# Attention and a token/channel mixer on one core: q and k loaded with 18 tokens per partition, one transfer per four heads

## The chip, the cores and the metric

The kernel runs on one core of one Trainium2 chip. The metric is the device time of one execution in microseconds, given as the median of the runs of a kernel. The profile records one more execution; its span, from the first to the last instruction, is a little shorter than its device time.

## The reference

```python
# B = 8, H = 8, S = 576, D = 64; d_tok = 256, d_ch = 1536; all inputs and the output are float32
scores = 1/sqrt(D) * q @ k.T                       # per batch and head
bias   = -(cum[i] - cum[j]),  cum = cumsum(max(s, 0))
scores = where(j > i, -1e9, scores + min(bias, 0))
attn   = softmax(scores);  x = attn @ v            # x: (8, 576, 512) once the heads are side by side
h = relu(x^T @ w_tok1) @ w_tok2;   u = x + h^T     # mixes tokens
out = u + relu(u @ w_ch1) @ w_ch2                  # mixes channels
```

## The kernel before

**Tiling.** The batches are done one after the other. In a batch the eight heads are taken as two groups of four ("quads", qd = 0, 1). Four heads with 32 rows each fill the 128 partitions: a head's 64 columns are cast to bf16, two neighbouring columns are read as one fp32 word, and VectorE's 32x32 block transpose of these words (line 617) puts 32 words on 32 partitions, with the tokens along the free axis. TensorE then forms the scores with matmuls on 32 rows, two for each head and block (line 638, the two halves of each word). ScalarE takes the exponential (657), VectorE masks the diagonal blocks (662, 670), TensorE multiplies with v (692), VectorE normalises (699, 704). The bias enters as exp(cum), multiplied into v (line 553, on GpSimd from batch 1 on). Only neighbouring blocks of 128 tokens are multiplied; a check at the end selects a general path if the data don't allow that, and for it ScalarE squares and sums all of q and k (line 579, tile `junk`). For batches 0 and 1 that check loads q and k a second time (`stage_sq`), so there are 40 quad loads in all.

After the attention of a batch come the token mixer (`tok`: lines 759, 780, and the transposes of u: on TensorE at 805 with copies at 813 and 815 for batches 0 and 1, as DMA transposes at 796 from batch 2 on) and the channel mixer (`chan`: 833, its eviction with ReLU on ScalarE at 840 or VectorE at 842, then 851, the sum at 862, the store at 867 and 870).

**The loads.** `load_quad` (line 568) brings q or k of four heads in fp32 into one of four `qkf` buffers. With R = 2 a partition gets two neighbouring tokens (512 bytes) at a time, nine times, so each head is one DMA over 32 partitions with 288 runs of 512 bytes. Heads 0 and 1 are issued on SP (`load_op`, chained in order), heads 2 and 3 on ScalarE's queue (`load_op2`, chained likewise). A load waits for its `qkf` buffer, that is for the cast (591, 593 or 595, into one of four `qkn` buffers) of the load four before it; a cast in turn waits for its `qkn` buffer, which the transpose and, from batch 2 on, the square have to leave. v comes on SP, five DMAs a batch, in runs of 256 bytes (line 544), into two `vf` buffers. The weights come through GpSimd's queue, with a cast in flight (716). SP also carries the stores and the DMA transposes.

**What sets the order.** `Plan` takes all operations with assumed costs, simulates them on the engines with one number for the DMA time of a load, and emits each engine's instructions in the order of the planned starts. Each engine, and each issuing queue, then runs its own list strictly in order. An instruction that waits holds up everything behind it on that engine. Where the plan sees TensorE idle in its first 95 us, `fills` puts in matmuls on zeros (line 937), to keep TensorE's clock up.

Of the kernel before, what the change touches and what calls it, by code (L numbers as in the profile page):

```python
# [213 lines left out]
def c_act(n, bias=False):  # L214
    occ = 0.07 + n * 0.000833 + (0.093 if bias else 0.0)
    return occ, occ + 0.22
# [7 lines left out]
def c_pool(n, per=0.0022):  # L224
    occ = 0.10 + n * per
    return occ, occ + 0.25
# [111 lines left out]
def kernel(  # L338
# [12 lines left out]
    nc = tc.nc  # L351

    B, H, S, D = q.shape
# [8 lines left out]
    LAG = 2.0  # L362
    WARM = 95.0
    TOK = 2.0
    R = 2

    const = ctx.enter_context(tc.tile_pool(name="const", bufs=1))
    fast_ctx = ExitStack()
# [50 lines left out]
    P = Plan()  # L419
    last = [None]  # L420

    def load_op(fn, key, us):

        last[0] = P.op({"SP": (0.42, 0, fn)}, writes=key, prio=1, dma=us, after=last[0])

    last2 = [None]

    def load_op2(fn, key, us):

        last2[0] = P.op({"ACT": (0.42, 0, fn)}, writes=key, prio=0, dma=us, after=last2[0])  # L430


    nc.vector.memset(zero[:, :], 0.0)  # L433
# [20 lines left out]
    for i in range(1, 3):  # L454
        P.op({"DVE": (1.0, 1.2, lambda i=i: pads(nc.vector, i)), "POOL": (1.6, 1.8, lambda i=i: pads(nc.gpsimd, i))},
             writes=[("pad", i)], prio=40)
    P.op({"DVE": (0.6, 0.8, lambda: pads2(nc.vector)), "POOL": (1.0, 1.2, lambda: pads2(nc.gpsimd))},
         writes=["padw"], prio=41)
    P.op({"DVE": (0.3, 0.5, lambda: pads3(nc.vector, 1)), "POOL": (0.5, 0.7, lambda: pads3(nc.gpsimd, 1))},
         writes=["padv"], prio=42)  # L460
# [15 lines left out]
    def act(n, fn, bias=False):  # L476
# [4 lines left out]
         reads=["s"], writes=["sr"], prio=-1)  # L481
    P.op({"DVE": (1.3, 1.6, lambda: nc.vector.tensor_tensor_scan(
        out=cum[:, :], data0=one_sb[:, :], data1=s_sb[:, :], initial=0.0, op0=ALU.mult, op1=ALU.add))},
        reads=["sr"], writes=["cum"], prio=-1)
    P.op(dve(1, lambda: nc.vector.tensor_scalar(
        out=half[:, :], in0=cum[:, S - 1 : S], scalar1=-0.5, scalar2=None, op0=ALU.mult)),
        reads=["cum"], writes=["half"], prio=-1)
    P.op(act(576, lambda: nc.scalar.activation(
        out=wn[:, 0:S], in_=cum[:, :], func=AF.Exp, bias=half[:, 0:1], scale=1.0), True),
        reads=["half", "cum"], writes=["wn"], prio=-1)  # L490
    bw = Buf(r_mx, False)

    def w_tr():
# [6 lines left out]
        out=wT[:, :, :].rearrange("p c e -> p (c e)"), in_=bw.t[:, 0:384])),  # L500
        reads=[(bw, 0)], writes=["wT"], prio=-1)
# [18 lines left out]
        out=pre[:, :], data0=one_sb[:, :], data1=wn[:, 0:S], initial=0.0, op0=ALU.mult, op1=ALU.add))},  # L520
        reads=["wn"], writes=["pre"], prio=50)
# [44 lines left out]
    qkn, castop = {}, {}  # L566

    def load_quad(src, b, qd):
        f = Buf(r_qf)
        for g in (0, 2, 1, 3):  # L570
            on, eng = (load_op, nc.sync) if g < 2 else (load_op2, nc.scalar)
            on(lambda g=g, eng=eng: eng.dma_start(  # L572
                out=f.t[32 * g : 32 * g + 32, :].rearrange("p (k n) -> p k n", n=R * D),
                in_=src[b, 4 * qd + g, :, :].rearrange("(k p r) d -> p k (r d)", p=32, r=R)),
                [(f, g)], S / R * 0.027 / 16)
        return f

    def square(src, reads, col):
        P.op({"ACT": (1.2, 1.6, lambda: nc.scalar.activation(  # L579
            out=junk[:, :], in_=src.t[:, :], func=AF.Square, accum_out=sq[:, col : col + 1]))},  # L580
            reads=reads, writes=[("sq", col)], prio=60)

    def stage_qk(b, qd):
        for i, src in enumerate((k, q)):
            n = Buf(r_qn)
            qkn[(b, qd, i)] = n
            f = load_quad(src, b, qd)

            def cast(e, f=f, n=n):
                if e == 0:  # L590
                    nc.gpsimd.tensor_copy(out=n.t[:, :], in_=f.t[:, :])  # L591
                elif e == 1:
                    nc.vector.tensor_copy(out=n.t[:, :], in_=f.t[:, :])
                else:
                    nc.scalar.copy(out=n.t[:, :], in_=f.t[:, :])
            alts = {"POOL": (*c_pool(1152, 0.0010), lambda cast=cast: cast(0))}
            if b == 0 and (qd, i) != (1, 0):
                alts["DVE"] = (0.82, 1.04, lambda cast=cast: cast(1))
                alts["ACT"] = (*c_act(1152), lambda cast=cast: cast(2))
            castop[(b, qd, i)] = P.op(alts, reads=[(f, g) for g in range(4)], writes=[(n, 0)],  # L600
                                      prio=b * 10 + 4 * qd if b else 0)
            if b >= 2:
                square(n, [(n, 0)], (b * 2 + qd) * 2 + i)

    def stage_sq(b, qd):
        for i, src in enumerate((k, q)):
            f = load_quad(src, b, qd)
            square(f, [(f, g) for g in range(4)], (b * 2 + qd) * 2 + i)

    xbuf = {}  # L610

    def quad(b, qd):
        pads = [("pad", 1)] if b == 0 and qd == 1 else []
        qT, kT = Buf(r_qT), Buf(r_kT)
        for i, dst in ((0, kT), (1, qT)):
            n = qkn[(b, qd, i)]
            P.op(dve(576, lambda n=n, dst=dst: nc.vector.transpose(  # L617
                out=dst.t[:, 0:S, :].rearrange("d t e -> d (t e)").bitcast(FP32).rearrange(
                    "d (k p r) -> d k r p", p=32, r=R),
                in_=n.t[:, :].bitcast(FP32))), reads=[(n, 0)] + (pads if i == 0 else []), writes=[(dst, 0)], prio=1)  # L620
# [198 lines left out]
    def chan(b, u, us, uT):  # L819
# [26 lines left out]
        for ci, c in enumerate((4, 0, 1, 2, 3) if odd else (0, 1, 2, 3)):  # L846
# [24 lines left out]
            P.op({"SP": (0.45 if c < NJ - 1 else 0.9, 0, st)}, reads=[(o, 0)], prio=0, dma=128 * 0.088 / 16)  # L871

    stage_qk(0, 0)
    stage_v(0)
    stage_qk(0, 1)
    load_tok()
    stage_qk(1, 0)
    for i in range(4):
        load_ch1(i)
# [9 lines left out]
    for b in range(2):  # L889
        for qd in range(2):  # L890
            stage_sq(b, qd)
    for b in range(B):
        for qd in range(2):
# [5 lines left out]
        out=bad[:, 4:], in0=sq[:, :], scalar1=21.0, scalar2=None, op0=ALU.is_gt)),  # L899
        reads=[("sq", i) for i in range(NSQ)] + ["bad0"], writes=["bad"], prio=50)  # L900
# [3 lines left out]
         reads=["bad"], writes=[(bf, 0)], prio=(100, 0))  # L904
# [17 lines left out]
    for o in [o for o in order if o.eng == "PE"]:  # L922
# [3 lines left out]
        while t1 - t0 > 0.06:  # L926
            n = min(512, max(128, int((t1 - t0) * 2400)))
# [5 lines left out]
            if not slots:  # L933
                break
            f = Op()
            f.start, f.idx = t0, 0
            f.fn = lambda t=r.tiles[slots[0]], n=n: nc.tensor.matmul(  # L937
                out=t[:, 0:n], lhsT=zero[:, 0:128], rhs=zero[:, 0:n], start=True, stop=True)
# [47 lines left out]
```

## Time and profile before

| | us |
|---|---|
| median of 3 runs | 357.3 (356.89 to 360.31) |
| the profiled execution: its time | 357.3 |
| its span | 355.4, mean granted TensorE clock 0.945 |
| TensorE busy | 311.4, of it 35.6 in fills (line 937) in the windows of 20 us |
| VectorE / ScalarE / GpSimd busy | 196.1 / 159.8 / 86.9 |
| cast on GpSimd, L591, x29 | 34.8, 1220 ns each |
| block transposes, L617, x32 | 24.4, 771 ns (kT) and 756 ns (qT) each |
| q and k loads: DMAs | 160 of 144 KB, median 4.5 to 5.0 us from issue to landing |
| v loads | 32 of 256 KB and 8 of 128 KB, 6.9 and 6.4 us |

The profiled execution's time and the median of the runs agree. Busy times are of work alone: an engine that waits, or whose queue holds a DMA issue that waits, is counted as idle. "ACTq" and "SPq" in an answer are the issuing queues of ScalarE and SP; an issue that stands there is an instruction in that engine's list.

### The profile page before, as it was taken

The page shows a single profiled execution, that of the slowest core. Times are in us where ns is not written, and L with a number is a line of the kernel's source. Part 1 is how long each engine was busy: PE and PEld are TensorE (multiplying, and loading weights), DVE is VectorE, ACT ScalarE, POOL GpSimd, SP SyncE. Part 2 cuts the span into 40 slices and gives each one's busy share as a digit, 9 for nine tenths or more (in the row PEclk, how much of TensorE's full clock was granted, in tenths as well). Part 3 has the DMA queues.
Part 4 walks back from the last instruction along what each step waited for, and adds up shares of the span by engine and source line. Part 5 has one row for each costly group of instructions (what it writes and reads, how often), then busy time and mean ns, then how long its engine had stood idle before and what let it go on. Part 6 is the DMA issues. An engine that isn't in the chain of part 4 may idle for free.

```text
span 355.4 us, 6731 instructions
## 1 busy us (share of the span) xinstructions
PE 311.4 (88%) x2611; PEld 169.8 (48%) x2611; DVE 196.1 (55%) x422; ACT 159.8 (45%) x251; POOL 86.9 (24%) x110
## 2 busy tenths in 40 slices
PE   5896815999998499795999999999999999999992
PEld 1354414845555264342445754444467454546640
DVE  5576321738799288381196739587954454441021
ACT  0254104825562571633444745479467316414700
POOL 3167046603362092020620262025000000000000
PEclk9699686999999699898999999999999999999999
DMA  9999999379989969999059926986420231033021
GB/s 193 212 195 215 206 215 210 64 161 228 202 142 224 165 136 185 190 188 234 9 88 209 228 70 130 260 228 156 90 76 0 47 103 62 3 88 104 3 89 66
DMA packets 109640, 50.45 MB, mean 142 GB/s; under 512 B 55904, under 2 KB 104416, under 8 KB 109600
## 3 DMA queue, kind: packets, MB, share of 16 engines
q1 hardware_dynamic: 81872, 34.37, 47.1%
q10 hardware_dynamic: 24320, 11.80, 17.4%
q0 software_dynamic: 3408, 3.77, 6.3%
q8 instruction: 22, 0.36, 0.5%
q14 instruction: 18, 0.15, 0.2%
HBM read 40.71 MB, written 9.44 MB: 141 GB/s over the span
## 4 chain that ended last, share of the span: by engine, by line
PE 53%; DMA 13%; DVE 5%; SPq 4%; ACT 2%; issue 2%; POOL 1%; ACTq 0%; DVEq 0%; POOLq 0%
PE pmx L851 21%; PE pmx L833 21%; DMA vf<-in_v_dram 10%; DMA qkf<-in_k_dram 3%; PE pmx L759 3%; PE pav L692 3%; SPq L544 3%; PE psc L638 3%; PE pmx L780 2%; ACT junk L579 1%; DVE E L662 1%; DVE E L670 1%; SPq L572 1%; ACT E L657 1%; DVE kT L617 1%
## 5 line engine op out<-in xcount | busy, mean ns | idle before, releaser
L657 ACT ACTIVATE E<-psc 128x1024 bf16<-128x1024 f32 x64 | 62.0, 1021 | 46.0 <-PE psc L638 37.4
L833 PEld LDWEIGHTS <-wc 128*128 128x128 bf16 x624 | 59.8, 100 | 45.5 <-issue 16.2
L833 PE MATMUL pmx<-uTb,wc 128*128 128x320 bf16 x384 | 58.4, 305 | 6.9 <-ACT gb L840 6.3
L591 POOL CAST qkn<-qkf 128x1152 bf16<-128x1152 f32 x29 | 34.8, 1220 | 91.2 <-ACT E L657 36.1
L851 PE MATMUL pmx<-wc,gb 128*128 128x512 bf16 x240 | 56.8, 388 | 0.0
L833 PE MATMUL pmx<-uTa,wc 128*128 128x512 bf16 (+1 forms) x240 | 47.5, 348 | 4.4 <-ACT ga L840 3.8
L553 POOL TENSOR_TENSOR vp<-vf,wT 128x512 bf16<-128x512 f32 (+1 forms) x35 | 37.1, 1081 | 53.4 <-PE pav L692 22.0
L851 PE MATMUL pmx<-wc,ga 128*128 128x512 bf16 x192 | 45.2, 379 | 0.1
L662 DVE TENSOR_TENSOR E<-E,keep 128x512 bf16<-128x512 bf16 x64 | 37.2, 584 | 14.2 <-ACT E L657 13.8
L579 ACT ACTIVATE junk<-qkn 128x1152 bf16<-128x1152 bf16 x24 | 27.9, 1163 | 35.7 <-DMA vf<-in_v_dram 13.5
L840 ACT ACTIVATE gb<-pmx 128x320 bf16<-128x320 f32 x64 | 27.7, 437 | 29.8 <-PE pmx L833 22.0
L692 PEld LDWEIGHTS <-E 128*128 128x128 bf16 x576 | 26.2, 98 | 20.8 <-issue 5.1
L851 PEld LDWEIGHTS <-gb 128*128 128x128 bf16 x240 | 22.9, 99 | 26.5 <-issue 2.3
L692 PE MATMUL pav<-vp,E 128*128 128x65 bf16 x540 | 27.8, 195 | 7.9 <-DVE E L662 3.1
L937 PE MATMUL pmx<-zero 128*128 128x512 bf16 (+5 forms) x114 | 32.2, 427 | 1.2 <-DVE zero L433 1.2
L704 DVE TENSOR_TENSOR x<-pav,rc 128x320 bf16<-128x320 f32 x60 | 29.5, 491 | 1.9
L840 ACT ACTIVATE ga<-pmx 128x512 bf16<-128x512 f32 (+1 forms) x39 | 19.4, 504 | 20.3 <-PE pmx L833 19.7
L851 PEld LDWEIGHTS <-ga 128*128 128x128 bf16 x192 | 17.7, 98 | 19.8 <-issue 0.9
L699 DVE RECIPROCAL rc<-pav 128x5 f32<-128x5 f32 x60 | 11.2, 187 | 24.6 <-PE pav L692 24.3
L638 PE MATMUL psc<-qT,kT 32*128 32x256 bf16 (+2 forms) x640 | 23.1, 253 | 0.1
L862 DVE TENSOR_TENSOR of<-pmx,ua 128x512 f32<-128x512 f32 x16 | 11.0, 690 | 21.7 <-PE pmx L851 14.8
L842 DVE TENSOR_SCALAR ga<-pmx 128x512 bf16<-128x512 f32 (+1 forms) x21 | 12.3, 595 | 18.7 <-PE pmx L833 18.7
(82 smaller groups left out, 255.6 us busy)
## 6 DMA issues: line engine op xcount, KB each, us to landing
vf<-in_v_dram SPq DMA_DIRECT2D x32, 256.0 KB, 6.9
out_dram<-of SPq DMA_DIRECT2D x32, 256.0 KB, 2.4
qkf<-in_k_dram ACTq DMA_DIRECT2D x40, 144.0 KB, 5.0
qkf<-in_k_dram SPq DMA_DIRECT2D x40, 144.0 KB, 4.7
qkf<-in_q_dram ACTq DMA_DIRECT2D x40, 144.0 KB, 4.5
qkf<-in_q_dram SPq DMA_DIRECT2D x40, 144.0 KB, 4.7
wc<-in_moe_w_ch_dram POOLq DMA_DIRECT2D x8, 384.0 KB, 11.7
vf<-in_v_dram SPq DMA_DIRECT2D x8, 128.0 KB, 6.4
```

The costliest lines, as they stand in the source:

```text
L553: eng.tensor_tensor(out=vp.t[p0 : p0 + n, c, :, 0:D], in0=vf.t[p0 : p0 + n, c, :, :], in1=wT[p0 : p0 + n, cw, b * H : b * H + H].unsqueeze ...
L579: P.op({"ACT": (1.2, 1.6, lambda: nc.scalar.activation(out=junk[:, :], in_=src.t[:, :], func=AF.Square, accum_out=sq[:, col : col + 1]))}, ...
L591: nc.gpsimd.tensor_copy(out=n.t[:, :], in_=f.t[:, :])
L638: nc.tensor.matmul(out=pss[g // 2].t[:, g % 2, c0 : c0 + z - a], lhsT=kT.t[rows, j0 : j0 + 128, e], rhs=qT.t[rows, a:z, e], start=(e == 0) ...
L657: nc.scalar.activation(out=E.t[:, :, gi * 512 : gi * 512 + 512], in_=ps.t[:, :, :], func=AF.Exp, scale=0.125)
L662: nc.vector.tensor_tensor(out=o, in0=o, in1=keep[:, :].unsqueeze(1).unsqueeze(1).to_broadcast([128, 2, 2, 128]), op=ALU.mult)
L692: nc.tensor.matmul(out=o[:, ic, 0 : D + 1], lhsT=E.t[:, hh, d0 : d0 + 128], rhs=vp.t[:, jc, h + hh, 0 : D + 1], start=(jc == j_lo), stop=( ...
L704: nc.vector.tensor_tensor(out=x.t[:, :, (h + hh) * D : (h + hh + 1) * D], in0=o[:, :, 0:D], in1=rc.t[:, :].unsqueeze(2).to_broadcast([128, ...
L833: nc.tensor.matmul(out=pm.t[:, 0 : e - a], lhsT=wc1[:, m, cc * 128 : cc * 128 + 128], rhs=uT.t[:, m, a:e], start=(m == 0), stop=(m == NMC ...
L840: lambda cc=cc, pm=pm, a=a, e=e: nc.scalar.activation(out=g.t[:, cc, a:e], in_=pm.t[:, 0 : e - a], func=AF.Relu),
L851: nc.tensor.matmul(out=pm.t[:, :], lhsT=g.t[:, cc, c * 128 : c * 128 + 128], rhs=wc2[:, cc, :], start=(cc == 0), stop=(cc == NCC - 1))
L937: f.fn = lambda t=r.tiles[slots[0]], n=n: nc.tensor.matmul(out=t[:, 0:n], lhsT=zero[:, 0:128], rhs=zero[:, 0:n], start=True, stop=True)
```

## The change

R becomes 18: a partition gets 18 neighbouring tokens of one head, 4608 bytes in one run, and 32 partitions hold a head. The four heads of a quad are then 128 partitions of one contiguous piece of DRAM, and the load is one DMA, on SP. The issues on ScalarE's queue and `load_op2` go. The transpose's output pattern, which is written in terms of R, follows: within a block of 32 tokens it wrote every second word (8 bytes apart), and it now writes every 18th (72 bytes apart). What lies in `kT` and `qT` afterwards is the same as before. The planner is told 1.52 us of DMA time for a quad (128 x 0.19 / 16) where four times 0.486 us stood, and ScalarE's list has no issues.

```diff
-    R = 2
+    R = 18
...
-    last2 = [None]
-
-    def load_op2(fn, key, us):
-
-        last2[0] = P.op({"ACT": (0.42, 0, fn)}, writes=key, prio=0, dma=us, after=last2[0])
-
...
     def load_quad(src, b, qd):
         f = Buf(r_qf)
-        for g in (0, 2, 1, 3):
-            on, eng = (load_op, nc.sync) if g < 2 else (load_op2, nc.scalar)
-            on(lambda g=g, eng=eng: eng.dma_start(
-                out=f.t[32 * g : 32 * g + 32, :].rearrange("p (k n) -> p k n", n=R * D),
-                in_=src[b, 4 * qd + g, :, :].rearrange("(k p r) d -> p k (r d)", p=32, r=R)),
-                [(f, g)], S / R * 0.027 / 16)
+        load_op(lambda: nc.sync.dma_start(
+            out=f.t[:, :], in_=src[b, 4 * qd : 4 * qd + 4, :, :].rearrange("g (p r) d -> (g p) (r d)", r=R)),
+            [(f, 0)], 128 * 0.19 / 16)
         return f
...
-            castop[(b, qd, i)] = P.op(alts, reads=[(f, g) for g in range(4)], writes=[(n, 0)],
+            castop[(b, qd, i)] = P.op(alts, reads=[(f, 0)], writes=[(n, 0)],
...
-            square(f, [(f, g) for g in range(4)], (b * 2 + qd) * 2 + i)
+            square(f, [(f, 0)], (b * 2 + qd) * 2 + i)
```

The planner orders anew with these numbers. On each engine the instruction counts of the main path change as follows: the fills on TensorE go from 125 to 93; ScalarE loses its 80 issues, and takes 9 evictions of L842's kind and 3 of L770's kind from VectorE; VectorE's one cast goes to GpSimd; SP has 40 issues for q and k in place of 80. The order on TensorE changes in places, its other work does not.

## The prediction

> **What bounds the kernel now.** I read the page first, then TensorE's waits from 40 to 180 us, then ScalarE's timeline at the places where these waits point.
>
> The page's slices: TensorE, its granted clock, and the DMA engines, 8.9 us to a digit.
>
> ```profile
> PE   5896815999998499795999999999999999999992
> ...
> PEclk9699686999999699898999999999999999999999
> DMA  9999999379989969999059926986420231033021
> ```
>
> From slice 20 (178 us) on TensorE is busy at full clock until the end; nothing there can be won by feeding it better. The loss lies before: digits of 1, 4 and 5 with a clock of 6 to 8 beside them. The DMA engines are busy for most of the first 165 us, but the next view says that a transfer is not what TensorE itself waits for.
>
> TensorE's waits from 40 to 180 us (total us, times, longest):
>
> ```profile
> PE pmx L805 <- ACT uTa L813: 10.9, 1, 10.9
> PE pmx L833 <- ACT gb L840: 6.3, 2, 5.2
> PE pmx L833 <- ACT ga L840: 3.8, 1, 3.8
> PE pav L692 <- DVE x L704: 3.0, 3, 2.7
> ```
>
> Nearly all are waits for a copy on ScalarE that empties PSUM. ScalarE is only 45% busy, so why are the copies late? Its timeline (start, length, idle time ahead in brackets; ACTq is an issue on ScalarE's own queue):
>
> ```profile
> 39.88 13.17 ACTq L572 DMA_DIRECT2D qkf<-in_k_dram  x2
> 54.38 1.95 ACTq L572 DMA_DIRECT2D qkf<-in_q_dram  x2
> 56.43 2.05 ACT L813 COPY uTa<-pmx 128x512 bf16<-128x512 bf16 x4 [16.03 <-DMA qkf<-in_k_dram]
> ...
> 119.33 0.32 ACTq L572 DMA_DIRECT2D qkf<-in_k_dram  x1
> 119.69 1.16 ACT L579 ACTIVATE junk<-qkn 128x1152 bf16<-128x1152 bf16 x1 [5.69 <-DMA vf<-in_v_dram]
> ...
> 163.39 0.83 ACTq L572 DMA_DIRECT2D qkf<-in_q_dram  x2
> 164.26 1.16 ACT L579 ACTIVATE junk<-qkn 128x1152 bf16<-128x1152 bf16 x1 [6.19 <-DMA out_dram<-of]
> 165.42 1.55 ACT L840 ACTIVATE ga<-pmx 128x512 bf16<-128x512 f32 x3
> ```
>
> The four copies of uTa stand in ScalarE's list behind four issues of q and k loads. These take or wait from 39.88 to 56.33 us, and the copies start at 56.43, though TensorE had written the data at about 46. At 113 to 121 and at 162 to 166 the same happens: an issue that waits for its buffer stands in front of the gb and ga evictions. At 145 to 148 the issue at 145.72 stands in front of the exponential at 146.08, from which the x of the fourth row follows. So what bounds the first half is loads that wait inside an engine whose next work TensorE needs.
>
> **The change part by part.** All sums are made against the span of 355.4 us; the execution's time is 357.3, 1.9 more, and equals the median of the runs.
>
> *ScalarE's issues go.* The gaps behind them are 10.9, 6.3, 2.7 (the long one of the fourth row) and 3.8 us, 23.7 in all. The copies themselves remain: in each of the five places about 0.5 us (0.44 for gb, 0.60 for ga and uTa) passes before TensorE can go on, so 23.7 - 2.7 = 21. What is late next? At 46 us the matmuls L833 need wc1; the gate issue on SP, which waits for the first part of wc2, ran at 41.2 and wc1 was issued ahead of wc2, so the weights are there. The v of batch 1 was multiplied by 54.9 us for a product that TensorE reached at 78, and the casts of batch 2's first quad were done by 62.6 for scores at 91: 11 us less leaves both early. At 116 the v of the next product was ready at 104 for 134. So I find nothing late within the gain.
>
> *The clock.* After these gaps TensorE ran at a granted 0.67 (57 to 62 us), 0.61 (122 to 126), 0.66 (148 to 153) and 0.72 (166 to 172). The loss is 5 x 0.33 + 4 x 0.39 + 5 x 0.34 + 6 x 0.28 = 6.6 us. I count 5 as won, since some gaps will stay.
>
> *Fills.* 32 fewer. Ten of them are before the first scores, where 23 took 7.36 us (0.32 each), 22 mostly between 84 and 98 us, where 9 took 1.94 (0.216 each): 3.2 + 4.8 = 8 us. A fill costs nothing where the work behind it isn't ready, so the bounds are 0 and 8; TensorE hardly waited right behind the fills there (0.23 us), which speaks for the upper end. I take 6.
>
> *SP.* It issued 80 loads for 311 to 1562 ns each and now issues 40. The waits that ScalarE's queue carried stand on SP already, for the same buffers (heads 0 and 1 wait with heads 2 and 3), so SP gets no new one; behind a waiting load stand, as before, v, the stores and the DMA transposes of u. But the mutual order changes (a store of batch 0 now stands between the k and the q load of a quad), and a load on a single queue passes behind v's packets with all four heads. I charge 2 us, bounds 0 and 13 (half of the waits removed come back here).
>
> *Packets.* The rows that price them (packets, MB, share of 16 engines): the page's ScalarE queue, only q and k; and SP's queue from 322 to 355 us, stores of 2 KB with small packets.
>
> ```profile
> q10 hardware_dynamic: 24320, 11.80, 17.4%
> ...
> q1 hardware_dynamic: 1578, 1.97, 18.2%
> ```
>
> 0.174 x 16 x 355.4 / 24320 = 41 ns for one of 512 bytes, so a quad costs 1152 x 41 / 16 = 2.9 us of all engines. In the second row 0.182 x 16 x 33 = 96 us went to 896 packets of 2 KB (and 682 small ones), 107 ns at most; by bytes a packet of 4608 is 241 ns, a quad 128 x 241 / 16 = 1.9 us. Between 1.9 (near rows of large packets, taken) and 2.9 (no better by bytes) the 40 quads save 40 to 0 us of DMA time. None of it is on TensorE's path as shown above, so it enters at 0. Its cover is the lead of the loads over their use; if that is gone, it is worth up to 1 us a quad.
>
> *VectorE's transposes.* Same instruction, same elements, but writes 72 bytes apart in place of 8. No VectorE row has such a stride. The rows that bound it:
>
> ```profile
> L617 DVE STREAM_TRANSPOSE kT<-qkn x16: 737/772/781, 8.4 to 264.7; 128x576 f32<-128x576 f32 x16
> ...
> L561 POOL CAST vp<-wT 128x32 bf16<-128x32 f32 x8 | 2.5, 325 | 15.4 <-DVE wT L499 8.1 <-PE pav L692 6.2 <-PE pmx L692 1.0
> L563 POOL CAST vp<-wT 64x8 bf16<-64x8 f32 x8 | 2.0, 244 | 0.3
> ```
>
> From below, 0.77 us as now; a faster one is excluded, since VectorE's dense fp32 row at 553 (0.69 us for 512 elements) is no quicker an element. From above, GpSimd's two small casts write 132 bytes apart: (325 - 244) / (32 - 8) = 3.4 ns an element, and 576 x 3.4 + 0.17 = 2.1 us. Another engine, but the only rows with a stride like this. I take the middle, 1.4, because one end has the right instruction and the other the right stride: 32 x 0.63 = 20 us more on VectorE, which is 55% busy. The chain of waits has a kT or qT transpose at four places (183.07, 216.71, 233.41, 234.18), 4 x 0.63 = 2.5 us; with some crowding where VectorE is busy for 16 of 20 us (80 to 120), 4 us. Bounds: 0, and 32 x 1.35 = 43 if every one at 2.1 us is exposed.
>
> The Trainium skill speaks against this part: "SBUF — State Buffer", § Door 1, says that consecutive accesses within one 16-byte line go at full bandwidth, that at least two hits on a line are needed, and that an access to a new line each time pays a penalty. The old pattern has two words in a line and the new one has one. The trace shows 0.77 us for the old pattern, which agrees, and nothing for the new one. The page gives no size. Without that rule this term would be 0 and the forecast 4 us lower.
>
> The same skill speaks against a gain from the packets: "DMA: Bandwidth & Descriptors", § Specifications, has 512 bytes as the least transfer for line rate, so 4608 would save nothing of DMA time. The two rows above, 12.5 bytes a nanosecond against at least 19, differ from it. Since the term is 0 in the sum, both give the same forecast.
>
> *Sum:* 355.4 - 21 - 5 - 6 + 2 + 4 = 329.4 span, + 1.9 = **331 us**.
>
> **The rivals.**
>
> *B, the waits move.* The late thing is in truth the buffers (GpSimd's casts waited 47.7 us in all for loads and what stands before them), and with ScalarE free TensorE runs into the next wait, for a score or a v, or for a store that stands behind a load on SP. For it: the DMA engines are busy in nearly every slice up to 165 us. Against: the lead of 11 to 30 us found above. Price: half of the 26 us of gaps and clock come back, 331 + 13 = 344.
>
> *C, slower: VectorE's transposes.* At 2.1 us and with none hidden, 43 us in place of the 4: 331 - 4 + 43 = 370. It decides when (357.3 - 331 + 4) / 32 = 0.95 us more are exposed for each, that is from 1.7 us with no cover. For it: kT and qT have two buffers each, the transposes stand in one list with masks and normalisation, and TensorE's product waits on these. Against: VectorE is idle for 45% of the span and only four transposes are on the chain.
>
> *D, no change.* The planner's new order only trades one gap for another, for the same 355 to 359 us. For it: everything after 178 us is TensorE at full speed. Against: this needs 26 us of new waits in a stretch of 130 us.
>
> **How the numbers follow.** A 0.66, B 0.18, C 0.11, D 0.05. The time is A's, 331. Below, all bounds in its favour: 355.4 - 23.7 - 6.6 - 8 = 317.1 span, 319 us; I go to 317 for the startup. Above, B with a little more, 347; C and D lie outside. A and B are faster by over 1% (the three runs before spread over about 1%, so less can't be told from no change): faster 0.84, same 0.05, slower 0.11.
>
> **What would show it.** Right: no issues in ScalarE's list; TensorE's 10.9 us wait for uTa gone, the slices before 178 us without a 1; a granted clock above 0.945; L617 between 0.8 and 2.1 us; the loads of q and k landing no later after issue than 5 us. Wrong: TensorE waiting as long at the same places for scores or v (B), VectorE's kT or qT among TensorE's longest waits with L617 over 1.7 us (C), or a store or a DMA transpose on SP that waits behind a load.

## The result and the profile after

| | us |
|---|---|
| before, median | 357.1 (356.73 to 360.31) |
| after, median | 323.1 (321.15 to 323.81) |
| estimated ratio | 0.902, 95% interval 0.896 to 0.909 (the two medians alone: 0.905) |
| the profiled execution: time, span | 323.8, 322.0 |
| mean granted clock | 0.985 (0.945 before) |

34 us were gained where 26 were forecast; 323 lies inside the range. Line numbers after the edit are 6 to 9 lower: 617 is now 608, 638 is 629, 657 is 648, 813 is 804, 840 is 831, 937 is 928.

The page's slices, 8.05 us to a digit:

```profile
PE   6986989998899899997999999999999999999991
...
PEclk9799799999999999999999999999999999999998
DMA  7999988999995479402992387605101610141032
```

Up to the last slice the 1, the 4 and the 5s of TensorE are gone, and its clock falls only twice early on. TensorE's waits from 40 to 180 us (total, times, longest), the four longest:

```profile
PE pav L683 <- DVE E L661: 1.5, 2, 0.8
PE pav L683 <- DVE x L695: 1.3, 3, 0.5
PE pmx L824 <- DVE ga L833: 1.2, 2, 0.9
PE psc L629 <- DVE qT L608: 0.9, 2, 0.6
```

No wait for ScalarE is left, the longest is 0.9 us where it was 10.9, and every one of the four is for VectorE. ScalarE's timeline around the uTa copies, first the last h of before, then after, with no issue in it:

```profile
39.80 0.60 ACT L769 ACTIVATE h<-pmx 128x512 bf16<-128x512 f32 x1 [0.47 <-PE pmx L759]
```

```profile
33.56 0.60 ACT L760 ACTIVATE h<-pmx 128x512 bf16<-128x512 f32 x1 [0.47 <-PE pmx L750]
38.29 2.26 ACT L804 COPY uTa<-pmx 128x512 bf16<-128x512 bf16 x4 [4.14 <-PE pmx L796]
40.75 0.38 ACT L831 ACTIVATE ga<-pmx 128x256 bf16<-128x256 f32 x1 [0.20 <-PE pmx L824]
```

The copies start 4.7 us after the start of the last h and wait for TensorE (796); before, they started 16.6 us after it (39.80 to 56.43) and waited for a load.

The start, from which the prediction had read only the fills, gained too. The fills ahead of the first scores, and the first scores, before and after, from TensorE's timelines:

```profile
11.15 7.36 PE L937 MATMUL pmx<-zero 128*128 128x512 bf16 x23
18.44 1.09 PE L638 MATMUL psc<-qT,kT 32*128 32x256 bf16 x20
```

```profile
7.97 4.33 PE L928 MATMUL pmx<-zero 128*128 128x512 bf16 x12
12.23 1.08 PE L629 MATMUL psc<-qT,kT 32*128 32x256 bf16 x20
```

And ScalarE's first 10 us before:

```profile
0.76 0.89 ACTq L572 DMA_DIRECT2D qkf<-in_k_dram  x2
1.67 0.98 ACTq L572 DMA_DIRECT2D qkf<-in_q_dram  x2
3.91 0.97 ACTq L572 DMA_DIRECT2D qkf<-in_k_dram  x2
6.43 1.67 ACTq L572 DMA_DIRECT2D qkf<-in_q_dram  x2
8.13 1.28 ACT L488 ACT_TABLE_LOAD   x1 [8.13 <-DMA qkf<-in_k_dram]
9.43 0.78 ACT L488 ACTIVATE wn<-cum,half 64x576 f32<-64x576 f32 x1
```

Eight issues stood ahead of the table load and of the exponential of cum. It is the same stall as in the middle. It is not the whole gain: of the 6.2 us, 3.2 pass before these fills begin (11.15 against 7.97), and 3.0 are the fills themselves (23 in 7.36 us, 12 in 4.33), which the prediction had counted.

The two costs, from the tile answer for kT, the queue table and the chain of waits (before's chain is the last fence):

```profile
L608 DVE STREAM_TRANSPOSE kT<-qkn x16: 1235/1249/1260, 6.7 to 231.0; 128x576 f32<-128x576 f32 x16
```

```profile
q1 hardware_dynamic: 63312, 46.17, 51.2%
...
PE 65%; DVE 28%; issue 2%; ACT 2%; DMA 1%; SPq 0%; DVEq 0%
```

```profile
PE 53%; DMA 13%; DVE 5%; SPq 4%; ACT 2%; issue 2%; POOL 1%; ACTq 0%; DVEq 0%; POOLq 0%
```

A transpose takes 1.25 us where it took 0.77. VectorE now has 28% of the chain, where it had 5%; DMA has 1%, where it had 13%; the shares of before add up to only 80%, so they are compared roughly. One sign that the prediction had named for being right fails: the loads land 5.4 and 5.8 us after their issue, not within 5.

### The profile page after: what moved, and what is told of

Its sections match the earlier page's. It is cut to its first block, busy times and chain, and to the rows that moved or that the text cites. A ratio compares the mean times of both kernels' runs of the same rounds, so it can differ in the third digit from the quotient of the medians.

```text
span 322.0 us, 6476 instructions
## 1 busy us (share of the span) xinstructions
PE 297.7 (92%) x2579; PEld 164.3 (51%) x2579; DVE 199.4 (62%) x409; ACT 165.1 (51%) x263; POOL 88.2 (27%) x111
## 3 DMA queue, kind: packets, MB, share of 16 engines
q1 hardware_dynamic: 63312, 46.17, 51.2%
## 4 chain that ended last, share of the span: by engine, by line
PE 65%; DVE 28%; issue 2%; ACT 2%; DMA 1%; SPq 0%; DVEq 0%
PE pmx L842 25%; PE pmx L824 23%; DVE kT L608 5%; PE pmx L750 5%; DVE E L653 4%; PE psc L629 4%; PE pav L683 4%; DVE qT L608 4%; DVE E L661 3%; DVE x L695 3%; PE pmx L771 2%; DVE ub L778 2%; PE pmx L928 2%; DVE ga L833 1%; DVE ua L778 1%
## 5 line engine op out<-in xcount | busy, mean ns | idle before, releaser
L824 PEld LDWEIGHTS <-wc 128*128 128x128 bf16 x624 | 58.5, 98 | 34.5 <-issue 5.1
L582 POOL CAST qkn<-qkf 128x1152 bf16<-128x1152 f32 x30 | 35.6, 1203 | 81.7 <-ACT E L648 45.3
L824 PE MATMUL pmx<-uTb,wc 128*128 128x320 bf16 x384 | 56.3, 299 | 0.5 <-DVE gb L833 0.3
L842 PE MATMUL pmx<-wc,gb 128*128 128x512 bf16 x240 | 55.2, 379 | 0.8 <-DVE ua L778 0.8
L831 ACT ACTIVATE gb<-pmx 128x320 bf16<-128x320 f32 x74 | 32.4, 437 | 38.6 <-PE pmx L824 33.7
L824 PE MATMUL pmx<-uTa,wc 128*128 128x512 bf16 (+1 forms) x240 | 45.3, 337 | 1.2 <-DVE ga L833 1.2
L842 PE MATMUL pmx<-wc,ga 128*128 128x512 bf16 x192 | 45.9, 379 | 0.3
L842 PEld LDWEIGHTS <-gb 128*128 128x128 bf16 x240 | 22.5, 98 | 26.1 <-issue 1.5
L653 DVE TENSOR_TENSOR E<-E,keep 128x512 bf16<-128x512 bf16 x64 | 32.7, 515 | 4.9 <-ACT E L648 4.7
L831 ACT ACTIVATE ga<-pmx 128x512 bf16<-128x512 f32 (+1 forms) x38 | 19.1, 502 | 22.7 <-PE pmx L824 22.1
L842 PEld LDWEIGHTS <-ga 128*128 128x128 bf16 x192 | 17.4, 97 | 19.0 <-issue 1.2
L928 PE MATMUL pmx<-zero 128*128 128x512 bf16 (+3 forms) x82 | 23.8, 429 | 1.6 <-DVE zero L427 1.2
L608 DVE STREAM_TRANSPOSE kT<-qkn 128x576 f32<-128x576 f32 x16 | 20.0, 1251 | 6.9 <-PE psc L629 5.9
L853 DVE TENSOR_TENSOR of<-pmx,us 128x512 f32<-128x512 f32 x4 | 2.8, 692 | 33.0 <-PE pmx L842 33.0
## 6 DMA issues: line engine op xcount, KB each, us to landing
wc<-in_moe_w_ch_dram POOLq DMA_DIRECT2D x8, 384.0 KB, 12.2
```

What stands on the lines that cost most here:

```text
L608: P.op(dve(576, lambda n=n, dst=dst: nc.vector.transpose(out=dst.t[:, 0:S, :].rearrange("d t e -> d (t e)").bitcast(FP32).rearrange("d (k ...
L653: nc.vector.tensor_tensor(out=o, in0=o, in1=keep[:, :].unsqueeze(1).unsqueeze(1).to_broadcast([128, 2, 2, 128]), op=ALU.mult)
L824: nc.tensor.matmul(out=pm.t[:, 0 : e - a], lhsT=wc1[:, m, cc * 128 : cc * 128 + 128], rhs=uT.t[:, m, a:e], start=(m == 0), stop=(m == NMC ...
L831: lambda cc=cc, pm=pm, a=a, e=e: nc.scalar.activation(out=g.t[:, cc, a:e], in_=pm.t[:, 0 : e - a], func=AF.Relu),
L842: nc.tensor.matmul(out=pm.t[:, :], lhsT=g.t[:, cc, c * 128 : c * 128 + 128], rhs=wc2[:, cc, :], start=(cc == 0), stop=(cc == NCC - 1))
L928: f.fn = lambda t=r.tiles[slots[0]], n=n: nc.tensor.matmul(out=t[:, 0:n], lhsT=zero[:, 0:128], rhs=zero[:, 0:n], start=True, stop=True)
```

## The experiments

Times are medians of four runs. They were taken in three sessions, each on another chip and each with runs of before beside them: experiments 1 to 4 (median of before 354.3), 5, 6, 7 and 9 (355.5), 8 and 10 (356.8). The changed kernel ran only earlier, beside a before of 357.1. So a time of one session can be off by up to some 3 us against that of another. Where this matters, the gain over the before beside is given too; the changed kernel's is 34.0 us.

**1. Only the place of the issue.** The load of before, all on SP, with every engine's order as planned before:

```diff
-            on, eng = (load_op, nc.sync) if g < 2 else (load_op2, nc.scalar)
+            on, eng = (load_op, nc.sync) if g < 2 else (load_op2, nc.sync)
```

> As before, with every engine's order kept as the planner of before made it (it still counts the issues on ScalarE), only that SP's sequencer issues what ScalarE's did, in the same places of the plan. Theory 1: 357 less 23.7 us of gaps, less 2.7 us for the evictions, less 5 us of clock, so 331, within 5. Theory 2: 350 or more. Theory 3 (the planner's new order is the gain): no change, 355 to 359.

332.1 us (330.0 to 332.3), ratio 0.937 [0.929, 0.945]. No packet, no transpose and no place in the plan's order has changed, and about 22 us are gone: Theory 1 holds, Theories 2 and 3 fall as the main cause. First scores came at 14.34 us. What changes with the issuing engine is only that all loads go through SP's queue. Two new waits show: 2.7 us for the token mixer's weights, and the one that the prediction named under SP:

```profile
PE pmx L833 <- DMA uTa<-ua: 7.4, 1, 7.4
```

SP's timeline ahead of it:

```profile
115.08 2.20 SPq L544 DMA_DIRECT2D vf<-in_v_dram  x2
117.38 1.56 SPq L572 DMA_DIRECT2D qkf<-in_k_dram  x3
119.04 0.90 SPq L572 DMA_DIRECT2D qkf<-in_q_dram  x2
119.98 0.45 SPq L572 DMA_DIRECT2D qkf<-in_k_dram  x1
120.48 0.95 SPq L572 DMA_DIRECT2D qkf<-in_q_dram  x2
121.53 2.67 SPq L572 DMA_DIRECT2D qkf<-in_k_dram  x4
124.50 0.31 SPq L572 DMA_DIRECT2D qkf<-in_q_dram  x1
125.26 1.45 SPq L870 DMA_DIRECT2D out_dram<-of  x2
126.75 1.10 SPq L572 DMA_DIRECT2D qkf<-in_q_dram  x2
127.96 5.25 SPq L796 DMA_TRANSPOSE uTa<-ua  x4
```

VectorE had ua ready at 116.2 us; its DMA transposes were issued from 127.96, behind loads and two stores. So part of the stall did move from ScalarE to SP, as rival B said. But no one issue that waits for its buffer makes up this delay: the rows show SP issuing for some 10.5 of these 11.8 us. It simply has many issues ahead of the transposes.

**2. The same with a new plan.**

```diff
-            on, eng = (load_op, nc.sync) if g < 2 else (load_op2, nc.scalar)
+            on, eng = (load_op, nc.sync)
```

> The load of before (R = 2, four DMAs of 512-byte runs a quad, transposes that write 8 bytes apart), but all four issued on SP; the planner orders anew. Theory 1 (issues that wait inside ScalarE's list hold up its evictions): most of the gain comes, 320 to 333 us, L617 at 0.77 us, TensorE's 10.9 us wait for uTa gone. Theory 2 (the long runs of 4608 bytes feed TensorE sooner): 345 us or more, since the DMA engines are no faster. If Theory 1 is right and the transposes' longer time costs the new kernel much, this one is even under 323.

323.7 us (322.2 to 324.3): by the times within 1 us of the changed kernel, by the gain over the before beside (30.6) 3.4 us short of it, with neither its long runs nor its slow transposes (0.77 us here). The planner, now knowing that ScalarE has no issues, gives 8.4 us over experiment 1. The fills fall from 125 to 107, and TensorE's long waits for uTa, 10.9 us in before and 7.4 in experiment 1, are gone; its longest is now

```profile
PE pav L692 <- DVE E L670: 4.4, 4, 2.5
```

**3. Only the long runs, issues split as before.** R = 18, and the planner's DMA number for a load of one head `32 * 0.19 / 16`:

> R = 18, so long runs and transposes that write 72 bytes apart, but four DMAs a quad (32 partitions each), two on SP and two on ScalarE's queue as before. Theory 1: ScalarE's issues still wait in front of its evictions: 345 to 360 us, the wait of TensorE for uTa still several us. Theory 2: 318 to 328, as the new kernel.

344.7 us (344.4 to 345.9), just under the range that Theory 1 gave. The stall is there; ScalarE's timeline:

```profile
48.22 1.16 ACTq L572 DMA_DIRECT2D qkf<-in_k_dram  x2
52.13 2.15 ACTq L572 DMA_DIRECT2D qkf<-in_q_dram  x2
54.38 1.56 ACT L813 COPY uTa<-pmx 128x512 bf16<-128x512 bf16 x3 [12.22 <-DMA qkf<-in_k_dram]
```

TensorE waited 7.7 us for it. Long runs alone, net of slow transposes and with their own plan, bring some 10 us (ratio 0.975, interval 0.968 to 0.983, so 6 to 11): a third of the whole, and not nothing, which the sum had.

**4. The price of the stride.** In the changed kernel, writes 8 bytes apart, tokens of kT and qT in another order:

```diff
-                    "d (k p r) -> d k r p", p=32, r=R),
+                    "d (k p r) -> d k r p", p=32, r=2),
```

> The changed kernel, except that the transposes write every second word as before, so the tokens of kT and qT lie in another order and the scores mix tokens (this part of the computation is changed; amounts of work are the same). It prices the stride by itself: L608 falls from 1.25 to 0.77 us. By the prediction's term (0.63 us each, 4 us on the path) scaled to the measured 0.48: 3 us, so 320. By the chain of waits of the changed kernel, where kT and qT stand at more than 20 places: 20 x 0.48 = 10 us, so 313. If the path takes none: 323.

315.6 us (313.9 to 316.4), with

```profile
L608 DVE STREAM_TRANSPOSE kT<-qkn 128x576 f32<-128x576 f32 x16 | 12.3, 770 | 7.1 <-PE psc L629 6.0 <-ACT qkn L586 1.1
```

By the times the stride costs 7.5 us, by the gains over the before beside (38.7 against 34.0) 4.7: between the 3 that the prediction's term gave and the 10 of the chain. Against experiment 2, which has dense writes too and ran in the same session, the long-run load with its plan is worth 8.1.

**5 and 6. Distance or line?** R = 3 and R = 6, with four DMAs on SP as in experiment 2 (the planner's packet numbers 0.036 and 0.066).

> R = 3, four DMAs a quad on SP: runs of 768 bytes, transposes that write 12 bytes apart, so of four words in 48 bytes two share a 16-byte line and two have one alone. If a word alone in its line is what costs (line theory), L617 takes 0.77 + half of 0.48 = 1.0 us; if the distance costs, in proportion to it, 0.80. Time by interpolation between R = 2 on SP (323.7) and R = 18: 318 to 326.

> R = 6, four DMAs a quad on SP: runs of 1536 bytes, transposes that write 24 bytes apart, each word in a line of its own. Line theory: L617 takes 1.25 us, as with 72 bytes. Distance theory: 0.77 + 0.48 x 16 / 64 = 0.89. Time: with 1.25 us 321 to 327; with 0.89 318 to 322.

323.7 us (322.1 to 324.6) and 325.6 (322.8 to 326.8). The transposes, R = 3 and then R = 6, from the groups of VectorE (busy us, mean ns):

```profile
L617 DVE STREAM_TRANSPOSE kT<-qkn 128x576 f32<-128x576 f32 x16 | 15.4, 961 | 8.9 <-PE psc L638 5.7 <-ACT qkn L595 3.2
```

```profile
L617 DVE STREAM_TRANSPOSE kT<-qkn 128x576 f32<-128x576 f32 x16 | 19.5, 1219 | 8.9 <-PE psc L638 5.7 <-ACT qkn L595 3.2
```

At 24 bytes nearly all of the price is paid (1.22 of 1.25), at 12 some 40% of it (0.96). That fits the line theory (1.0 and 1.25 expected); by distance R = 6 would take 0.89. A price that grows with the distance and stops growing by 24 bytes is not excluded, since no run writes 4 or 16 bytes apart. The Trainium skill's rule ("SBUF — State Buffer", § Door 1) agrees with this trace: the step lies between 8 and 24 bytes, where a 16-byte line no longer holds two words. Its size, 0.48 us on 576 words, is the runs'. Neither beats experiment 2.

**7. An order that knows.** The changed kernel with the planner counting 1.25 us for a transpose:

```diff
-            P.op(dve(576, lambda n=n, dst=dst: nc.vector.transpose(
+            P.op(dve(1135, lambda n=n, dst=dst: nc.vector.transpose(
```

> The changed kernel, only that the planner counts 1.25 us for a transpose in place of 0.67, so it orders VectorE's list with the time that was measured. If the 7.5 us that the stride costs are exposed because the order is made for a shorter transpose, some of them come back: 318 to 321. If VectorE is simply full where they stand, 322 to 325.

315.0 us (314.2 to 316.3), ratio 0.8875 [0.883, 0.892], below the changed kernel's interval. That is better than either range expected. One number in the planner brings 8.1 us by the times, 6.5 by the gains (40.5 against 34.0), as much as the stride costs, with transposes as slow as they were (1.25 us). The chain of waits:

```profile
PE 73%; DVE 12%; ACT 6%; DMA 4%; issue 3%; POOL 0%; SPq 0%; DVEq 0%; ACTq 0%; POOLq 0%
```

VectorE's share falls from 28% to 12% with no less work.

**8. Is it the number's truth, or only room?** The changed kernel told 0.96 us (`dve(855, ...`), then experiments 4 and 2 told 1.25, which is too long there:

> The changed kernel with the planner told 0.96 us, halfway between 0.67 and the true 1.25. Truth and slack theory alike: 317 to 321, between 323 and 315. Scatter theory: outside of that.

> The long-run load with dense writes (transposes of 0.77 us; tokens of kT and qT in another order, as in that run) and the planner told 1.25 us, which is now too long. Truth theory (the order was made for too short a transpose, and told the truth it recovers): told wrong the other way, it gains nothing over 315.6, or loses: 314 to 320. Slack theory (any order that gives the transposes more room is better): 307 to 312. If the planner's orders simply scatter, anything between 308 and 328.

> R = 2, four DMAs on SP, transposes of 0.77 us, the planner told 1.25. Truth theory: 322 to 328, no better than 323.7. Slack theory: 314 to 319.

| transposes take | load | told 0.67 | told 0.96 | told 1.25 |
|---|---|---|---|---|
| 1.25 | long runs | 323.1, gain 34.0 | 316.2 (315.9 to 317.1), gain 40.6 | 315.0, gain 40.5 |
| 0.77 | long runs | 315.6, gain 38.7 | | 313.4 (311.9 to 315.4), gain 43.4 |
| 0.77 | R = 2 on SP | 323.7, gain 30.6 | | 321.3 (321.1 to 321.6), gain 35.5 |

The gains are over the median of before in the same session; each step along a row goes from one session to another. Told 1.25, the kernel with slow transposes is 8.1 us faster by the times and 6.5 by the gains. The two with fast transposes, for which 1.25 is too long, are 2.2 and 2.4 us faster by the times, and 4.7 and 4.9 by the gains. So room alone, with a number that isn't true, brings at least 2 us and perhaps most of it; how much is truth stays open. Both fell between the ranges of the two theories, and the number halfway, which brings 6.6 to 6.9 us, came out 0.8 us below the range that both gave it. Under the longer number the stride costs 1.6 us (315.0 against 313.4, whose runs overlap), 2.9 by the gains.

The R = 2 kernel told 1.25 also shows where the long runs' 8 us lie: in the same session its long-run twin takes 8.0 us less. The chain of waits of R = 2, then of the twin, and a wait of TensorE with R = 2:

```profile
PE 63%; DMA 13%; DVE 8%; SPq 6%; issue 4%; ACT 3%; POOL 1%; ACTq 0%; DVEq 0%; POOLq 0%
```

```profile
PE 72%; DVE 9%; ACT 7%; DMA 4%; issue 4%; POOL 0%; SPq 0%; ACTq 0%; DVEq 0%; POOLq 0%
```

```profile
PE pmx L833 <- DMA uTa<-ua: 4.1, 1, 4.1
```

The twin has first scores at 13.9 us in place of 16.4, no wait of TensorE for uTa, and DMA 4% and SP 0% of its chain. So here the long runs gain at the start, and by a shorter queue ahead of the DMA transposes. Between experiments 2 and 4 the gain looks otherwise: there the first scores come at 15.4 and 12.2, no wait for uTa stood in experiment 2, and TensorE's time in fills falls from 29.7 to 24.1 us.

**9. Transfer or plan?** The changed kernel, the planner told the old DMA time of a load (`4 * 288 * 0.027 / 16`):

> The changed kernel, only that the planner counts for a quad load the 1.94 us of DMA time of before in place of 1.52. The 8 us between the R = 2 load on SP (323.7) and the long-run load with dense writes (315.6) are either the transfers themselves (packet theory: then this run stays at 321 to 325) or the planner's other order (plan theory: then it goes to 328 to 331).

327.1 us (325.4 to 328.2), between the two theories. It is 4.0 us more than the changed kernel by the times and 5.6 by the gains (28.4 against 34.0). So of the 8 us some 4 to 6 go with what the planner is told of the load, and the rest may be the transfers themselves. This split is rough: told numbers move the order by 2 us and more also where they aren't true (experiment 8).

**10. A mix.** R = 18 in one DMA for batch 0 and for the check's second loads, R = 2 in four DMAs on SP elsewhere, the planner told 1.25 and 0.77:

> Long runs (R = 18, one DMA) only where they may pay: batch 0, which starts the pipeline, and the eight loads of the check, which have no transpose; elsewhere R = 2 in four DMAs on SP, with transposes of 0.77 us. The planner is told each. If long runs pay mainly at the start (first scores at 12.2 us in place of 15.4) and dense transposes later, 312 to 318, as good as or better than the 315 of the long-run kernel that knows its transposes; if the 144 KB transfers of the middle cost, 319 to 324.

318.3 us (317.3 to 319.4), between the two ranges: 3 us better than R = 2 throughout with room (321.3, same session), and 4.9 us worse than long runs with fast transposes throughout (313.4, same session). So the loads of the middle, with the order that is made for them, count too.

## Why the prediction was right, and which terms were mis-sized

- *ScalarE's issues (21) and the clock (5):* 26 forecast, 22 measured against the runs beside it (354.3 to 332.1 in experiment 1), 25 against the first session's median of before. That the main cause is the place of the issue is shown. But the sum agrees better than its terms, and that is luck: the first scores came 4.1 us earlier (18.44 to 14.34), which no term had, and the DMA transposes behind SP's loads took 7.4 back. The clock rose to 0.970 there and to 0.985 after.
- *Fills (6):* TensorE's time in fills fell from 35.6 to 27.1 us in the windows, 8.5. But experiment 1, with all 125 fills, has only 32.3 left, at its higher clock. From there the new plan of experiment 2 takes away 2.6 us of fills and gives 8.4 in all; the 7.4 us wait for uTa went with it. So some 2.6 of its 8.4 are fills, and 5.6 more of fills go at the next step, the long runs (24.1 us with 93 fills, in experiment 4).
- *SP (2, bounds 0 and 13):* the forecast's reason, that SP gets no new wait, was wrong as it stands. With R = 2 SP has 160 loads to issue, twice those of before, and under the old order TensorE waits 7.4 us for the DMA transposes behind them; with one DMA a quad that wait is not there, nor is it in experiment 2 with its own order (experiment 8's R = 2 has 4.1 of it).
- *Packets (0):* the step that failed. The price was right. With long runs SP's queue has the 51.2% shown above, and in experiment 2

```profile
q1 hardware_dynamic: 106192, 46.17, 63.1%
```

  That is: 51.2% of 322 us against 63.1% of 321.4, so 607 engine-us less, 0.95 us of all 16 for each of 40 quads, where 1.0 was worked out. That none of it is on TensorE's path was wrong: the long runs with their plan are worth 8.1 us between experiments 2 and 4, and 8.0 between the two kernels of experiment 8, whose fills take almost the same time (28.1 and 27.2 us). Reading TensorE's waits only from 40 to 180 us hid the start, and reading which wait ended last on TensorE in the old kernel could not show what would end last once ScalarE was out of the way.
- *Transposes (4):* 1.4 us taken, 1.25 measured, so the middle between two unlike rows was near, by luck: neither row prices what experiments 5 and 6 show. The path took 4.7 to 7.5 while the planner counted 0.67, and 1.6 to 2.9 with 1.25.
- *Sum by the runs:* -25 (place of the issue, with the clock), -8.4 (new plan), -8.1 (long runs), +7.5 (stride): -34.0. This is one chain from before to after, so it must come to the measured 34, and its first and last step go from one session to another; by the gains the steps are -22.1, -8.4, -8.1 and +4.7. The 8 us missing from the forecast stand at the step of the long runs, but as 5.6 us of fills go there too, and the start and SP's wait stand in other steps, another way of taking the steps could share them out otherwise.
- *Rivals.* B was half right: a wait did move to SP, one of any size only for R = 2. C has its mechanism (VectorE in place of ScalarE) and no more than 7.5 of its 43 us. D is out.

## What to carry to other kernels

A DMA issue that waits for a buffer holds up everything behind it on its engine: put it on an engine whose next work nobody waits for, and look on that engine for the next thing that it then delays. When an edit changes what an instruction costs, try the planner's number, too: here one number brought 6.5 to 8 us, about as much as the long transfers. Try it also where it isn't true before you call it the truth that helped. A term that is set to zero because the path doesn't show it should be checked at the start of the kernel and under the path that the edit leaves, not only under the old one.

## What was not expected of the hardware

VectorE's 32x32 transpose of 576 fp32 words takes 0.77 us with writes 8 bytes apart, 0.96 at 12, 1.22 at 24 and 1.25 at 72: beyond 24 bytes the distance costs next to nothing more. And two kernels as unlike as R = 2 on SP (four DMAs, fast transposes) and R = 18 (one DMA, slow ones) came out at 323.7 and 323.1, in two sessions, by opposite terms of 5 to 8 us.
